# Reading a recurrent memory in products of 136 columns instead of a numerator and a denominator apart

## The chip, the cores and the metric

The kernel runs on one core of a Trainium2 chip. The metric is the device time of one execution in microseconds (us), as the median of several runs. A core has five engines that run their own instruction streams and wait for each other through semaphores: TensorE (PE in the profile, with its weight loads as PEld), VectorE (DVE), ScalarE (ACT), GpSimd (POOL) and SyncE (SP), which here only starts DMA transfers. TensorE writes its products into PSUM; VectorE and ScalarE read them from there.

## The reference

Two blocks read the same input `x` (2048 tokens of 512 numbers, bf16), and a gate per token mixes their outputs. Block A is attention with a memory: the tokens are cut into four segments of 512, there are 32 heads of 16 numbers, and each segment attends to itself causally and also reads a matrix `M` and a vector `z` that the earlier segments left.

```
for s in range(4):
    qs, ks, vs = q[:, :, s], k[:, :, s], v[:, :, s]
    p = softmax(qs @ ks^T * scale + mask)
    a_dot = p @ vs
    pq = phi(qs)
    num = einsum('bhld,bhde->bhle', pq, M)
    den = einsum('bhld,bhd->bhl', pq, z)[..., None] + 1e-06
    o = g * (num / den) + (1 - g) * a_dot
    pk = phi(ks)
    M = M + einsum('bhld,bhle->bhde', pk, vs)
    z = z + einsum('bhld->bhd', pk)
a = concat(o) @ wo                      # g = sigmoid(beta), phi(t) = t + 1 or exp(t)
b = (gelu(x @ w_gate) * (x @ w_up)) @ w_down
out = gx * a + (1 - gx) * b             # gx = sigmoid((x * gate_w).sum())
```

The memory of segment 0 is zero, so only segments 1 to 3 read it.

## The kernel before

Features lie on the partitions. The 32 heads are four groups `c` of eight heads, which fill the 128 partitions. For a segment, `QT`, `ktb` and `pq` hold the transposed queries, keys and phi of the queries, 512 tokens along the free side.

The attention of a group (a "lump") goes over 8 blocks of 64 keys. The work is cut into 72 visits, which the text calls periods 1 to 72: each computes the logits `lg` of one or two blocks (L653, four PSUM banks, one tile), takes their exponential on ScalarE (L658, `pT`), and clears what lies above the diagonal on GpSimd (L662). Two periods after its last block, the group's product with V goes into two PSUM tiles `od` (L678). VectorE turns them into `oq` (L684), a period or two later `norm` divides them by the sums of values (L689, L690, L692), `back` turns them to `oT` (L697), and `add_mem` adds what was read from the memory (L700).

All other products are units that fill the rest of TensorE's time in each period: `kT`, `qT`, `vT`, `zT` (projections), `gT` and `uT` (gate and up), `dT` (down, 14 products of 512 columns into one tile), `aT` (the output). Each writes one PSUM tile of one bank through `gen`, and VectorE or ScalarE then copies it out. The pool behind `gen` has four banks. A tile takes over the bank of an earlier one, and its first product waits until that one's readers are done. `od` takes two banks.

The order of the instructions is fixed when the program is built. A planner keeps an estimate of TensorE's and ScalarE's time (`t_pe`, `t_act`) and of VectorE's backlog (`passed(pe, dve)`), and starts units from the streams until the period's goal is reached (`fill_to`); `later(n, f)` puts a step n periods on; `room_for_bank` counts the banks taken while a unit is open, and finishes the unit after the third. A changed cost or a changed count of tiles therefore moves units everywhere. After period 72 the planner runs a stretch of fill, then the last lump (`od`, norm, back, add), then all that is left.

The memory: `memory(s)` adds a segment's sums to `Macc` (L566). `u_mask` spreads `Macc` into block-diagonal bf16 tiles, `Mz` for z (L582) and `Mn` for M (L574, four VectorE instructions a segment in two halves, two and eight periods later). `u_den` makes the denominators of two groups in one bank: eight products of 8 columns (L603, tile `zd`), then on VectorE the sum with 1e-6 (L610), a reciprocal (L613) and a product with the gate (L614), kept in `rdm`. `mem_num` makes a group's numerators: four products of 128 columns, one for each 128 tokens (L632, tile `mn`), one VectorE product with `rdm` (L636, `tm`), and a DMA transpose to `mT` (L644) on SP's queue, which also carries the output and the transposes of `pk`. `mem_num` of a group is asked for in the period before the group's last block, and issued in the middle of the next.

At the end, the four output units of segment 3 need all four groups in `oT`. Their first product that reads group 3 waits for the last L700.

Of the kernel before, what the change touches and what calls it, by code (L numbers as in the profile page):

```python
# [13 lines left out]
P = 128  # L14
# [39 lines left out]
def kernel(  # L54
# [44 lines left out]
    gh = const([P, H], F32, "gh")  # L99
# [114 lines left out]
    def setup_beta():  # L214
        eb = wk2.tile([P, H], F32, name="eb", tag="eb")
# [355 lines left out]
    def u_mask(s):  # L571
        def half(h0):
            for c in (h0, h0 + 1):
                nc.vector.tensor_tensor(  # L574
                    out=Mn[s % 2][:, c, :].rearrange("q (j p d) -> q j p d", j=4, p=2),
                    in0=Macc[:, c, None, :, 0:16].to_broadcast((P, 4, 2, DH)),
                    in1=bm[:, :, 0:16].rearrange("q (j p) d -> q j p d", j=4), op=ALU.mult)
            passed(0.0, 0.6)
            done["Mn", s] = count(("Mn", s)) + 1

        def f():
            nc.vector.tensor_tensor(  # L582
                out=Mz[s % 2][:, :, :].rearrange("q c (j p) -> q c j p", j=4),
                in0=Macc[:, :, None, :, 16].to_broadcast((P, NC8, 4, 2)),
                in1=bm[:, None, :, 16].to_broadcast((P, NC8, 8))
                .rearrange("q c (j p) -> q c j p", j=4), op=ALU.mult)
# [8 lines left out]
    def u_den(s, pair):  # L595
        def f():
            assert general_now[0] or ("q", s, 2 * pair) in ready
            T = gen("zd")
            Tv = T[:, 0:KT * 16].rearrange("p (q h) -> p q h", q=KT)
            for cc in range(2):  # L600
                c = 2 * pair + cc
                for qq in range(KT):
                    nc.tensor.matmul(Tv[:, qq, 8 * cc:8 * cc + 8],  # L603
                                     lhsT=pq[:, c, qq * P:(qq + 1) * P],
                                     rhs=Mz[s % 2][:, c, :], start=True, stop=True)
                if cc == 0:
                    yield 0.12
            h0 = 16 * pair
            r = rdm[s % 2][:, :, h0:h0 + 16]
            nc.vector.tensor_scalar_add(r, Tv, 1e-6)  # L610

            def f_inv():
                nc.vector.reciprocal(r, r)  # L613
                nc.vector.tensor_tensor(out=r, in0=r,  # L614
                                        in1=gh[:, None, h0:h0 + 16].to_broadcast((P, KT, 16)),
                                        op=ALU.mult)
                passed(0.0, 0.8)
                done["inv", s] = count(("inv", s)) + 1
            if general_now[0]:
                f_inv()  # L620
            else:
                later(1, f_inv)
            return 0.12
        return 0.24, 0.22, f

    tms = {}

    def mem_num(s, c):
        assert general_now[0] or (count(("Mn", s)) > c // 2 and count(("inv", s)) > c // 2)
        T = gen("mn")  # L630
        for qq in range(KT):
            nc.tensor.matmul(T[:, qq * P:(qq + 1) * P],  # L632
                             lhsT=pq[:, c, qq * P:(qq + 1) * P], rhs=Mn[s % 2][:, c, :],
                             start=True, stop=True)
        tm = wk2.tile([P, KT, 8, DH], BF, name="tm", tag="tm")
        nc.vector.tensor_tensor(  # L636
            out=tm[:, :, :, :], in0=T[:, :].rearrange("p (q h d) -> p q h d", q=KT, h=8),
            in1=rdm[s % 2][:, :, 8 * c:8 * c + 8, None].to_broadcast((P, KT, 8, DH)), op=ALU.mult)
        mT = wk2.tile([P, L], BF, name="mT", tag="mT")
        mTv = mT[:, :].rearrange("p (q t) -> p q t", q=KT)  # L640
        if general_now[0]:
            turn(mTv, tm[:, :, :, :].rearrange("p q h d -> p q (h d)"))
        else:
            nc.sync.dma_start_transpose(mTv, tm[:, :, :, :].rearrange("p q h d -> p (q h d)"))  # L644
        tms[(s, c)] = mT
# [21 lines left out]
    def pv(s, c, blocks):  # L667
# [14 lines left out]
        oq = wk2.tile([P, 2, 16, 32], F32, name="oq", tag="oq", bufs=1)  # L682
        for p in range(2):
            nc.vector.transpose(oq[:, p, :, :].rearrange("p b r -> p (b r)"), od[p][:, :])  # L684
        return oq

    def norm(c, oq, o2):
        rden = wk2.tile([P, 2, 16], F32, name="rden", tag="rden")
        nc.vector.reciprocal(rden[:, :, :], oq[:, :, :, 16])  # L689
        nc.vector.tensor_tensor(out=rden[:, :, :], in0=rden[:, :, :],  # L690
                                in1=ogs[:, c, :, None].to_broadcast((P, 2, 16)), op=ALU.mult)
        nc.vector.tensor_tensor(  # L692
            out=o2[:, :, :, :].rearrange("q b p d -> q p b d"), in0=oq[:, :, :, 0:16],
            in1=rden[:, :, :, None].to_broadcast((P, 2, 16, DH)), op=ALU.mult)
# [279 lines left out]
    def can_num(s, c):  # L974
        if count(("den", s)) <= c // 2 and ("q", s, c - c % 2) in ready:
            need(("den", s), c // 2 + 1)
        return count(("Mn", s)) > c // 2 and count(("inv", s)) > c // 2

    asked = []
# [12 lines left out]
    for pieces in visits:  # L992
# [51 lines left out]
    assert not asked  # L1044
# [59 lines left out]
    def general():  # L1104
# [4 lines left out]
        for s in range(NSEG):  # L1109
# [16 lines left out]
            if s > 0:  # L1126
# [3 lines left out]
                run(u_den(s, 0))  # L1130
                run(u_den(s, 1))
# [4 lines left out]
            for c in range(NC8):  # L1136
                o2 = wk2.tile([P, 16, 2, DH], BF, name="o2", tag="o2")
                if s > 0:
                    mem_num(s, c)
# [66 lines left out]
```

## Time and profile before

| | |
|---|---|
| median of 3 runs | 267.97 us (267.69 to 268.17) |
| the profiled execution | 267.87 us, of which 266.1 us from the first to the last instruction (the span) |
| VectorE busy | 202.2 us, 380 instructions |
| ScalarE busy | 208.8 us |
| GpSimd busy | 156.7 us |
| granted clock of TensorE | 0.998 |

In the rows of the groups, a line reads: line of the kernel, engine, operation, output<-input, sizes, count, then busy time in us and mean duration of one in ns, then idle time before it with what ended it. In rows in order of time: start and duration in us, engine, line, operation, count. Where a row has a count over one, its duration runs from the first start to the last end. Ends of matmuls are modelled: a product of 512 columns shows 0.38 us, but the next one starts 0.216 us after it.

### The profile page before, as it was taken

The numbers are of one execution on the slowest core, as the hardware profiler recorded it, in microseconds if no ns is written. First come the engines' busy times: TensorE is split into PE (matmuls) and PEld (weight loads), VectorE is DVE, ScalarE is ACT, GpSimd is POOL, SyncE is SP. The second block draws the span as 40 slices with busy tenths as digits, with TensorE's granted clock in tenths as the row PEclk, the third lists the DMA queues.
The fourth block names the chain that finished last, engine by engine and source line by source line (L and its number), as shares of the span: only waits on it lengthen the run. The fifth ranks groups of instructions, "written<-read, shape, count | busy, mean of one in ns | idle before, by whom it ended". The sixth has DMA issues, their size and how long they took to land.

```text
span 266.1 us, 6868 instructions
## 1 busy us (share of the span) xinstructions
PE 261.3 (98%) x2865; PEld 117.3 (44%) x2865; DVE 202.2 (76%) x380; ACT 208.8 (78%) x162; POOL 156.7 (59%) x298
## 2 busy tenths in 40 slices
PE   7999999999999999999999999999999999999994
PEld 4454434344443444443445444444444444444442
DVE  2999574978669887789786888786979647696565
ACT  4236889988998899979899998788999988757610
POOL 3000158896716979887941988874795099745500
PEclk9999999999999999999999999999999999999999
DMA  6999941200322001301132011201010210002102
GB/s 200 348 182 286 304 111 39 42 4 0 69 58 42 2 0 42 79 5 21 22 79 47 0 23 39 60 5 22 1 43 22 46 23 18 4 20 42 41 22 84
DMA packets 30410, 16.60 MB, mean 62 GB/s; under 512 B 20008, under 2 KB 29096, under 8 KB 30376
## 3 DMA queue, kind: packets, MB, share of 16 engines
q1 hardware_dynamic: 30232, 16.07, 23.8%
q8 instruction: 23, 0.38, 0.6%
q14 instruction: 11, 0.09, 0.1%
q10 hardware_dynamic: 144, 0.07, 0.1%
HBM read 8.14 MB, written 2.10 MB: 38 GB/s over the span
## 4 chain that ended last, share of the span: by engine, by line
PE 96%; DVE 2%; issue 1%; DVEq 0%
PE uT L493 19%; PE gT L472 19%; PE dT L509 17%; PE lg L653 9%; PE od L678 7%; PE kT L375 5%; PE qT L289 5%; PE aT L532 5%; PE vT L413 5%; PE mn L632 1%; PE warm L166 1%; PE zT L429 1%; PE MT L560 1%; DVE tB L538 1%; PE x0T L183 1%
## 5 line engine op out<-in xcount | busy, mean ns | idle before, releaser
L662 POOL TENSOR_SCALAR_AFFINE_SELECT pT<-pT 64x256 bf16<-64x256 bf16 x256 | 114.0, 445 | 92.8 <-ACT pT L658 80.2
L658 ACT ACTIVATE pT<-lg 128x2048 bf16<-128x2048 f32 x72 | 135.1, 1876 | 23.6 <-PE lg L653 22.1
L493 PE MATMUL uT<-x,wup 128*128 128x512 bf16 x224 | 59.6, 380 | 0.0
L472 PE MATMUL gT<-x,wga 128*128 128x512 bf16 x224 | 56.7, 380 | 0.0
L509 PE MATMUL dT<-wdn,G 128*128 128x512 bf16 x224 | 53.6, 380 | 0.0
L499 DVE TENSOR_TENSOR G<-uT,G 128x512 bf16<-128x512 f32 x56 | 37.8, 681 | 8.7 <-PE uT L493 8.4
L385 POOL TENSOR_SCALAR KTm<-ktb,eo 128x512 bf16<-128x512 bf16 x26 | 40.6, 1574 | 1.3
L684 DVE STREAM_TRANSPOSE oq<-od 128x512 f32<-128x512 f32 x32 | 21.0, 695 | 19.0 <-PE od L678 19.0
L509 PEld LDWEIGHTS <-G 128*128 128x128 bf16 x224 | 20.4, 98 | 24.3 <-issue 3.0
L472 PEld LDWEIGHTS <-wga 128*128 128x128 bf16 x224 | 20.5, 98 | 23.9 <-issue 2.4
L493 PEld LDWEIGHTS <-wup 128*128 128x128 bf16 x224 | 20.1, 98 | 24.4 <-issue 4.3
L653 PE MATMUL lg<-QT,KTm 32*128 32x192 bf16 (+7 forms) x512 | 28.6, 287 | 0.0
L312 DVE CAST G<-gT 128x512 bf16<-128x512 f32 x25 | 17.1, 684 | 5.5 <-PE gT L472 5.2
L653 PEld LDWEIGHTS <-KTm 32*128 32x128 bf16 x512 | 8.4, 92 | 29.2 <-issue 29.1
L487 ACT ACTIVATE G<-G 128x3584 bf16<-128x3584 bf16 x6 | 18.8, 3182 | 0.0
L678 PE MATMUL od<-pT,V 64*32 64x128 bf16 (+7 forms) x512 | 18.8, 284 | 0.0
L678 PE MATMUL od<-pT,Vs 64*32 64x128 bf16 (+7 forms) x512 | 18.7, 284 | 0.0
L375 PE MATMUL kT<-x,wk 128*128 128x512 bf16 x64 | 16.6, 379 | 0.4 <-DVE eo L204 0.4
L532 PE MATMUL aT<-wo,oT 128*128 128x512 bf16 (+1 forms) x72 | 16.8, 356 | 0.1
L289 PE MATMUL qT<-x,wq 128*128 128x512 bf16 x64 | 16.6, 379 | 0.0
L538 DVE SCALAR_TENSOR_TENSOR tB<-aT,gct,tB 128x512 bf16<-128x512 f32 (+1 forms) x18 | 11.9, 680 | 5.2 <-PE aT L532 2.7
L678 PEld LDWEIGHTS <-V 64*32 64x32 bf16 x512 | 12.8, 92 | 6.0 <-issue 2.8
(96 smaller groups left out, 273.4 us busy)
## 6 DMA issues: line engine op xcount, KB each, us to landing
wup<-in_B_w_up_dram SPq DMA_DIRECT2D x1, 1792.0 KB, 10.1
wdn<-in_B_w_down_dram SPq DMA_DIRECT2D x1, 1792.0 KB
out_dram<-tB SPq DMA_DIRECT2D x13, 128.0 KB, 1.7
wga<-in_B_w_gate_dram SPq DMA_DIRECT2D x1, 1280.0 KB, 10.3
Vs<-V SPq DMA_DIRECT2D x8, 144.0 KB, 2.9
G<-in_A_x_dram SPq DMA_DIRECT2D x2, 256.0 KB, 2.8
wk<-in_A_wk_dram SPq DMA_DIRECT2D x2, 256.0 KB, 4.3
wq<-in_A_wq_dram SPq DMA_DIRECT2D x1, 512.0 KB, 5.6
```

The costliest lines, as they stand in the source:

```text
L289: nc.tensor.matmul(T[:, :], lhsT=wq[:, fc, c * P:(c + 1) * P], rhs=xS[s % NX][:, fc, :], start=(fc == 0), stop=(fc == FC - 1))
L375: nc.tensor.matmul(T[:, :], lhsT=wk[:, fc, c * P:(c + 1) * P], rhs=xS[s % NX][:, fc, :], start=(fc == 0), stop=(fc == FC - 1))
L385: eng.tensor_scalar(out=KTm[:, (NC8 * s + c) % NK, :, p, :], in0=ktb[:, c, :].rearrange("q (b k) -> q b k", b=NB), scalar1=eo[:, p:p + 1], ...
L472: nc.tensor.matmul(T[:, :], lhsT=wga[:, fc, hs * P:(hs + 1) * P], rhs=xS[s % NX][:, fc, :], start=(fc == 0), stop=(fc == FC - 1))
L493: nc.tensor.matmul(T[:, :], lhsT=wup[:, fc, hs * P:(hs + 1) * P], rhs=xS[s % NX][:, fc, :], start=(fc == 0), stop=(fc == FC - 1))
L499: nc.vector.tensor_tensor(out=g, in0=T[:, :], in1=g, op=ALU.mult)
L509: nc.tensor.matmul(T[:, :], lhsT=G[s % NG][:, hs, qt * P:(qt + 1) * P], rhs=wdn[:, hs, :], start=(hs == 0), stop=(hs == HS - 1))
L532: nc.tensor.matmul(T[:, 0:w], lhsT=oT[:, fc, qt * P:(qt + 1) * P], rhs=wo[:, fc, d0:d0 + w], start=(fc == 0), stop=(fc == FC - 1))
L653: nc.tensor.matmul(lg[:, j, off:off + n], lhsT=KTm[rows, i % NK, b].rearrange("r p k -> r (p k)"), rhs=QT[rows, i % NC8, 64 * b:L], start= ...
L658: nc.scalar.activation(pT[:, :, :], lg[:, :, :], AF.Exp, scale=DH ** -0.5)
L662: nc.gpsimd.affine_select(out=v, in_=v, pattern=[[0, 4], [1, 64]], compare_op=ALU.is_ge, fill=0.0, base=0, channel_multiplier=-1)
L678: nc.tensor.matmul(od[p][32 * j:32 * j + 32, 64 * b:L], lhsT=w[:, 18 * h:18 * h + 32], rhs=t[rows, j, off:off + n], start=(b == 0), stop=( ...
```

## The change

- The denominators are no longer products of their own: `Mn` gets 136 columns, 128 of M and 8 of z, and one product makes both. Three products fill a bank (408 of 512 columns), so a segment's 16 products go into six tiles (`mem_read`, m = 0 to 5) instead of four `mn` and two `zd`. A tile of three may straddle two groups.
- VectorE now works on each tile as it comes: the sum with 1e-6 times `eb` (which is 1 + exp(-beta), the inverse of the gate) in one instruction, a reciprocal, and the product that writes `tm`. Where a tile straddles two groups, the first and the last come twice.
- The reads are asked for at other periods, and the planner books (0.18, 1.1) us for each.
- The four copies of `Macc` into `Mn` go from VectorE to GpSimd, without a cost in the planner; the eight columns of z stay on VectorE.
- `oq` is laid out as (block, parity, number) instead of (parity, block, number), so that `norm` reads and writes in one order.

```diff
-    Mn = [const([P, NC8, 128], BF, f"Mn{i}") for i in range(2)]
-    Mz = [const([P, NC8, 8], BF, f"Mz{i}") for i in range(2)]
-    rdm = [const([P, KT, H], F32, f"rdm{i}") for i in range(2)]
+    Mn = [const([P, NC8, 136], BF, f"Mn{i}") for i in range(2)]
...
-                nc.vector.tensor_tensor(
-                    out=Mn[s % 2][:, c, :].rearrange("q (j p d) -> q j p d", j=4, p=2),
+                nc.gpsimd.tensor_tensor(
+                    out=Mn[s % 2][:, c, 0:128].rearrange("q (j p d) -> q j p d", j=4, p=2),
...
-            passed(0.0, 0.6)
...
+    def mem_read(s, m):
+        T = gen("mn")
+        todo = [divmod(t, KT) for t in range(3 * m, min(3 * m + 3, NC8 * KT))]
+        rd = wk2.tile([P, 3, 8], F32, name="rd", tag="rd")
+        parts = []
+        for i, (c, qq) in enumerate(todo):
+            nc.tensor.matmul(T[:, 136 * i:136 * i + 136], lhsT=pq[:, c, qq * P:(qq + 1) * P],
+                             rhs=Mn[s % 2][:, c, :], start=True, stop=True)
...
+        for c, qq, i, n in parts:
+            nc.vector.scalar_tensor_tensor(
+                out=rd[:, i:i + n, :], in0=Tv[:, i:i + n, 128:136], scalar=1e-6,
+                in1=eb[:, None, 8 * c:8 * c + 8].to_broadcast((P, n, 8)),
+                op0=ALU.add, op1=ALU.mult)
+        nc.vector.reciprocal(rd[:, 0:len(todo), :], rd[:, 0:len(todo), :])
+        for c, qq, i, n in parts:
...
+            nc.vector.tensor_tensor(
+                out=tm[:, qq:qq + n, :, :],
+                in0=Tv[:, i:i + n, 0:128].rearrange("p q (h d) -> p q h d", h=8),
+                in1=rd[:, i:i + n, :, None].to_broadcast((P, n, 8, DH)), op=ALU.mult)
...
+                nc.sync.dma_start_transpose(mTv, tm[:, :, :, :].rearrange("p q h d -> p (q h d)"))
...
-        oq = wk2.tile([P, 2, 16, 32], F32, name="oq", tag="oq", bufs=1)
+        oq = wk2.tile([P, 16, 2, 32], F32, name="oq", tag="oq", bufs=1)
         for p in range(2):
-            nc.vector.transpose(oq[:, p, :, :].rearrange("p b r -> p (b r)"), od[p][:, :])
+            nc.vector.transpose(oq[:, :, p, :], od[p][:, :].rearrange("q (b r) -> q b r", b=16))
...
         nc.vector.tensor_tensor(
-            out=o2[:, :, :, :].rearrange("q b p d -> q p b d"), in0=oq[:, :, :, 0:16],
-            in1=rden[:, :, :, None].to_broadcast((P, 2, 16, DH)), op=ALU.mult)
+            out=o2[:, :, :, :], in0=oq[:, :, :, 0:16],
+            in1=rden[:, :, :, None].to_broadcast((P, 16, 2, DH)), op=ALU.mult)
...
-        us += [unit(u_den(s + 1, pair), NP * s + 16 + 9 * pair, ("den", s + 1),
-                    lambda s=s, pair=pair: ("q", s + 1, 2 * pair) in ready)
-               for pair in range(2)]
...
-    def numerator(s, c):
+    def read(s, m):
         room_for_bank()
-        mem_num(s, c)
-        done["num", s] = count(("num", s)) + 1
-        passed(0.3, EVAC)
+        mem_read(s, m)
+        passed(0.18, 1.1)
...
+    reads = [(last(NC8 * s + c) - back_, s, m) for s in range(1, NSEG)
+             for c, back_, m in ((0, 1, 0), (0, 0, 1), (1, 0, 2), (2, 0, 3), (3, 1, 4), (3, 0, 5))]
...
-        for i in range(NC8, NSEG * NC8):
-            if last(i) - 1 == clock[0]:
-                asked.append((i // NC8, i % NC8))
-        if asked and can_num(*asked[0]):
-            pending.append(lambda a=asked.pop(0): numerator(*a))
+        if reads and reads[0][0] <= clock[0] and can_read(*reads[0][1:]):
+            pending.append(lambda a=reads.pop(0)[1:]: read(*a))
```

More of the change, by code (lines that the diff above doesn't have):

```diff
@@ L582, in f @@
             nc.vector.tensor_tensor(
-                out=Mz[s % 2][:, :, :].rearrange("q c (j p) -> q c j p", j=4),
+                out=Mn[s % 2][:, :, 128:136].rearrange("q c (j p) -> q c j p", j=4),
                 in0=Macc[:, :, None, :, 16].to_broadcast((P, NC8, 4, 2)),
@@ L593, in u_mask @@
         return 0.0, 0.2, f
[L595 to L618, printed above, removed]
+    tms = {}
@@ L619, in f @@
             if general_now[0]:
-                f_inv()
+                turn(mTv, tm[:, :, :, :].rearrange("p q h d -> p q (h d)"))
             else:
[L622 to L645, printed above, removed]
@@ L647, in group_qk @@
+                nc.sync.dma_start_transpose(mTv, tm[:, :, :, :].rearrange("p q h d -> p (q h d)"))
+            tms[(s, c)] = mT
+            done["num", s] = count(("num", s)) + 1
     def group_qk(pieces):
@@ L966, in lump, with can_read @@
             later(4, f_add)
-    def numerator(s, c):
+    def read(s, m):
         room_for_bank()
-        mem_num(s, c)
-        done["num", s] = count(("num", s)) + 1
-        passed(0.3, EVAC)
[L974 to L979, printed above, removed]
+        mem_read(s, m)
+        passed(0.18, 1.1)
+    def can_read(s, m):
+        cs = {t // KT for t in range(3 * m, min(3 * m + 3, NC8 * KT))}
+        return all(count(("Mn", s)) > c // 2 and ("q", s, c - c % 2) in ready for c in cs)
+    reads = [(last(NC8 * s + c) - back_, s, m) for s in range(1, NSEG)
+             for c, back_, m in ((0, 1, 0), (0, 0, 1), (1, 0, 2), (2, 0, 3), (3, 1, 4), (3, 0, 5))]
     pending = []
@@ L1137, in general @@
                 o2 = wk2.tile([P, 16, 2, DH], BF, name="o2", tag="o2")
-                if s > 0:
-                    mem_num(s, c)
+                for m in ((0, 1), (2,), (3,), (4, 5))[c] if s > 0 else ():
+                    mem_read(s, m)
                 tiles = {}
```

26 lines of the change are left out of this document (19 added, 7 removed).

## The prediction

> **What bounds the kernel now.** I read the page's span and busy times first, then its chain, the stretches, the waits, and last the end in order of time.
>
> ```profile
> span 266.1 us, 6868 instructions
> PE 261.3 (98%) x2865; PEld 117.3 (44%) x2865; DVE 202.2 (76%) x380; ACT 208.8 (78%) x162; POOL 156.7 (59%) x298
> PE 96%; DVE 2%; issue 1%; DVEq 0%
> 160.00:230.00 70.00, 70.00 (x852) 31.27 (x836) 52.99 (x102) 60.97 (x45) 49.57 (x90) 1.00 0.12 27
> ```
>
> The last row is a stretch (length, then busy time of PE, PEld, DVE, ACT, POOL, with counts, granted clock). In the middle TensorE is busy 70.00 of 70.00 us at full clock, so each product removed from its stream is time saved, and each wait of its stream is time lost. The one wait of size is at the end:
>
> ```profile
> PEld L532 <- DVE oT L700: 0.6, 1, 0.6
> 254.82 4.28 PE L509 MATMUL dT<-wdn,G 128*128 128x512 bf16 x19
> 255.00 1.31 DVE L684 STREAM_TRANSPOSE oq<-od 128x512 f32<-128x512 f32 x2 [2.30 <-PE od L678]
> 256.24 0.67 DVE L697 STREAM_TRANSPOSE oT<-o 128x512 bf16<-128x512 bf16 x1
> 256.94 0.43 DVE L700 TENSOR_TENSOR oT<-oT,mT 128x512 bf16<-128x512 bf16 x1
> 257.89 0.69 DVE L692 TENSOR_TENSOR o<-oq,rden 128x512 bf16<-128x512 f32 x1
> 258.94 3.91 PE L532 MATMUL aT<-wo,oT 128*128 128x512 bf16 x24
> 259.36 0.42 DVE L700 TENSOR_TENSOR oT<-oT,mT 128x512 bf16<-128x512 bf16 x1
> ```
>
> The last lump's `od` ends at 254.82. VectorE then works without a gap until the last L700 ends at 259.78 (259.36 + 0.42), 4.96 us later. Meanwhile TensorE has 19 `dT` products (254.82 to 258.94, 0.217 each) and three of `aT` (0.65), 4.77 us. The fourth `aT` reads the last group, so TensorE stands still for some 0.25 us there. The end is set by where this `od` lies.
>
> **What is removed from TensorE.**
>
> ```profile
> 141.59 0.34 PE L603 MATMUL zd<-Mz,pq 128*128 128x8 bf16 x8
> 141.79 0.38 PE L289 MATMUL qT<-x,wq 128*128 128x512 bf16 x1
> 109.29 0.40 PE L653 MATMUL lg<-QT,KTm 32*128 32x512 bf16 x4
> 109.62 0.26 PE L603 MATMUL zd<-Mz,pq 128*128 128x8 bf16 x4
> 109.85 0.38 PE L493 MATMUL uT<-x,wup 128*128 128x512 bf16 x1
> L632 PE MATMUL mn<-Mn,pq 128*128 128x128 bf16 x48 | 4.6, 219 | 0.0
> ```
>
> Eight denominators take 0.20 us from start to the next unit's start (141.79 - 141.59), so the 48 take 6 x 0.20 = 1.2 us. The one unit that was cut by a logits group cost more: its last four took 0.23 instead of 0.10, so with its other half I count 0.2 extra. Removed: 1.4 us. Added: 48 products of 136 instead of 128 columns, at 0.216/512 per column 48 x 8 x 0.00042 = 0.16. Net -1.25. Their cost can't be much off; TensorE's row shows it whole.
>
> **What moves at the end.** In the order that the changed code builds, written as unit and count of products, period 72 and what follows it reads:
>
> ```
> before  dT7 mn4 dT7 aT4 dT9 od64 dT19 aT24
> after   aT2 dT5 mn3 dT9 aT4 dT7 mn1 dT7 od64 dT14 aT24
> ```
>
> The second read (`mn1`) takes a bank while a `dT` unit is open. With the two banks of `od` that is the third, so `room_for_bank` finishes the unit ahead of `od`: five products that lay behind `od` now lie before it. Behind it remain 14 x 0.217 + 0.65 = 3.69 us for VectorE's same 4.96 us; the wait grows from 0.25 to about 1.3. `od` ends 5 x 0.217 = 1.08 later, and the end with it: +1.08. The read itself is no part of this: its VectorE work (0.75, below) and L644 behind it on SP's queue end well before the add, since `mn1` lies 2.7 us of TensorE ahead of the end of `od` (dT7 1.5, `od` 1.2) and the add another 4.5.
>
> **What VectorE pays.** Removed: L574, L610, L613, L614, L636.
>
> ```profile
> L636 DVE TENSOR_TENSOR tm<-mn,rdm 128x512 bf16<-128x512 f32 x12 | 8.2, 680 | 0.6 <-PE mn L632 0.4
> L574 DVE TENSOR_TENSOR Mn<-Macc,bm 128x128 bf16<-128x128 f32 x12 | 3.9, 366 | 0.0
> L613 DVE RECIPROCAL rdm<-rdm 128x64 f32<-128x64 f32 x6 | 3.1, 523 | 0.0
> L614 DVE TENSOR_TENSOR rdm<-rdm,gh 128x64 f32<-128x64 f32 x6 | 1.5, 256 | 0.2
> L610 DVE TENSOR_SCALAR rdm<-zd 128x64 f32<-128x64 f32 x6 | 1.3, 209 | 0.0
> L538 DVE SCALAR_TENSOR_TENSOR tB<-aT,gct,tB 128x512 bf16<-128x512 f32 x14 | 10.3, 739 | 5.2 <-PE aT L532 2.7 <-ACT pT L658 2.2
> L437 DVE CAST V<-zT 128x128 bf16<-128x128 f32 x8 | 1.9, 280 | 0.0
> L689 DVE RECIPROCAL rden<-oq 128x32 f32<-128x32 f32 x16 | 5.4, 340 | 0.0
> L442 DVE COPY gct<-zT 128x4 f32<-128x4 f32 x4 | 0.6, 151 | 0.0
> ```
>
> That is 18.0 us of busy time. Added, with no row of their own: the sum on 24 numbers lies between a copy of 4 (151 ns) and the sum of 64 (209); I take 0.22. The reciprocal of 24 is below that of 32 (340) and above a third of L613's (0.17); I take 0.29. The product of 384 lies between 128 (280) and 512 (680), on the line between them 0.55, of 256 0.41. A read in one part (m 0, 3, 4) is then 0.22 + 0.29 + 0.55 and two hand-overs of 0.03 (256.24 + 0.67 to 256.94 above), 1.13 us; one in two parts (m 1, 2) has five instructions and takes 1.32, since neighbours that don't wait for each other overlap by 0.07 (255.00 + 1.31 to 256.24); m 5, 0.75. Bounds for one part are 0.9 and 1.3. Per segment 3 x 1.13 + 2 x 1.32 + 0.75 = 6.8, in all 20.4: VectorE gains no room, it does 2 us more.
>
> That by itself is hidden, since VectorE is idle 24% of the time. What isn't hidden is the **bank**: `mn` was free after one instruction of 0.68, and now is after the whole read. The rows of the one place of before where an `od` follows an `mn` into its bank:
>
> ```profile
> 214.83 0.39 PE L632 MATMUL mn<-Mn,pq 128*128 128x128 bf16 x4
> 215.05 0.38 PE L375 MATMUL kT<-x,wk 128*128 128x512 bf16 x1
> 215.25 0.69 DVE L636 TENSOR_TENSOR tm<-mn,rdm 128x512 bf16<-128x512 f32 x1
> 216.01 0.40 PE L653 MATMUL lg<-QT,KTm 32*128 32x448 bf16 x8
> 216.34 0.39 PE L678 MATMUL od<-pT,V 64*32 64x512 bf16 x1
> ```
>
> VectorE starts 0.20 after the last product ends (215.05), frees the bank at 215.94, and `od` starts at 216.34, 1.29 after the products: 0.40 to spare. In the changed order, three `od` stand as close behind an `mn` whose bank they take (units between `mn` and the logits group):
>
> ```
> period 24   aT4 gT1 mn3 gT3 uT1   then lg, od64     (m 1, two parts)
> period 33   vT4 uT1 mn3 uT3 gT1   then lg, od64     (m 3, one part)
> period 69   uT5 mn3 uT2 dT2       then lg, od64     (m 3, one part)
> ```
>
> ```profile
> L312 DVE CAST V<-vT 128x448 bf16<-128x448 f32 x9 | 5.5, 616 | 0.4
> 114.87 1.31 DVE L684 STREAM_TRANSPOSE oq<-od 128x512 f32<-128x512 f32 x2 [0.49 <-PE od L678]
> 125.07 0.75 DVE L538 SCALAR_TENSOR_TENSOR tB<-aT,gct,tB 128x512 bf16<-128x512 f32 x1 [0.28 <-PE aT L532]
> ```
>
> In each 0.86 us of products and the logits group lie between, as above, so 1.27 from `mn` to `od`. In period 24 VectorE has first to finish L538 of the `aT` that ended 0.40 before (0.20 + 0.75, in turn, so it begins the read 0.47 after `mn`): 0.47 + 1.32 + 0.08 to be seen - 1.27 = a wait of 0.60. In period 33 the copy of `vT` (0.62) stands ahead, and the read begins 0.34 after: 0.34 + 1.13 + 0.08 - 1.27 = 0.28. In period 69 it begins at 0.2: 0.14. Together 1.0, and with the bounds of a read 0.4 to 1.7. TensorE runs in order: behind the `od` stands everything else, the next logits group and so ScalarE's exponentials too. In period 46 (m 2) the sums of z and M stand between as well, 1.7 us: hidden by 0.1, and the first to bind if VectorE is later than I think.
>
> **GpSimd's copies.** No row shows one; by its rows for 512 numbers (1.57 us) and 136 with one input (0.38) a copy of 128 lies between 0.38 and 1.57, nearer the smaller by its size: 0.5, two at a time 1.0.
>
> ```profile
> L385 POOL TENSOR_SCALAR KTm<-ktb,eo 128x512 bf16<-128x512 bf16 x26 | 40.6, 1574 | 1.3
> L200 POOL TENSOR_SCALAR_AFFINE_SELECT bm<-bm 128x136 bf16<-128x136 bf16 x1 | 0.4, 382 | 0.1
> 123.52 2.01 POOL L662 TENSOR_SCALAR_AFFINE_SELECT pT<-pT 64x256 bf16<-64x256 bf16 x4 [0.71 <-ACT pT L658]
> 126.59 0.39 PE L678 MATMUL od<-pT,V 64*32 64x512 bf16 x1
> ```
>
> Behind them on POOL wait L662 and L385, and `od` waits for L662. The last row shows 0.71 us idle ahead of the masks, and they end at 125.53, 1.06 before the `od` at 126.59: 1.0 fits into the idle time and that distance. Nothing counted; if a copy took 1.57, three `od` (periods 16, 34, 52) would each wait 3.1 - 0.7 - 1.06 = 1.35. The Trainium skill (GPSIMD Engine Reference, Engine selection) says that GpSimd is about twice as slow as VectorE where an operation has two inputs; by it, from VectorE's quiet 0.28, a copy is an estimated 0.55 and the sum stays as it is.
>
> **The norm's order.** I count nothing, in either direction:
>
> ```profile
> L692 DVE TENSOR_TENSOR o<-oq,rden x16: 691/926/945, 50.9 to 257.9; 128x512 bf16<-128x512 f32 x16
> ```
>
> The same instruction takes 0.69 or 0.94; 0.69 is the pace of other products of 512. If the order were what costs the 0.25, up to 16 x 0.24 = 3.8 us of VectorE would go, and the three waits with it; at the end it is already 0.69, so the tail can't gain. The Trainium skill (GPSIMD Engine Reference, Key points) says that GpSimd shares its SBUF interfaces with VectorE, which suffers where it has two SBUF inputs; the norm has two, in either order. By that rule it stays at 0.94; the last one, with GpSimd done, is the quick one.
>
> **Sum**, against the profiled execution (267.87 us: span 266.1 and 1.8 around it; 0.10 below the median of the runs): 267.87 - 1.25 + 1.08 + 1.0 = 268.7, on the median's scale 268.8.
>
> **Rivals.**
> 1. *No bank wait*, because VectorE is ahead at the three places or the norm gives it 0.25 a lump: 267.87 - 1.25 + 1.08 = 267.7, on the median's scale 267.8, no change. For: before's closest case had 0.40 to spare. Against: 1.13 and 1.32 are longer than 0.69 by just this.
> 2. *The saving stays*: no waits, and the end hidden, as it would be if VectorE's last chain were 1.1 shorter: 267.97 - 1.25 = 266.7. Against: 4.96 us without a gap, with the norm at its quick pace already.
> 3. *VectorE falls behind* by 0.6 at each place, the 2 us more coming where it is busiest: the three waits grow to 2.8, period 46 waits 0.5: 268.8 + 2.3 = 271.1. It decides once the read begins 0.5 later than I have it. For: after a lump it can run without a gap for ten us (the rows at 114.87 and 125.07, the next that was idle before).
> 4. *GpSimd holds the masks up*, at 1.57 a copy: 268.8 + 3 x 1.35 = 272.8.
>
> **Numbers.** The forecast 0.47 (its own range, by the bounds of a read, 268.2 to 269.5), rival 1 0.22, rival 2 0.10, rival 3 0.16, rival 4 0.05. Range: 267.2 leaves out rival 2, 270.4 most of 3 and all of 4, together under 0.25 as rival 3 reaches down to 270. About 0.2% (0.54 us) can be told from no change. Faster: rival 2 and a little of rival 1, 0.14; the same: the rest of rival 1 and the forecast's low end, 0.25; slower: the rest, 0.61.
>
> **What would show it.** The L603 rows of `zd` gone and `mn` at some 0.06 a product; TensorE's waits naming `tm` or VectorE ahead of `od` in periods 25, 34 and 70; L532 waiting about 1.3 us for L700 at the end with 14 `dT` ahead; L692 still between 0.69 and 0.94; GpSimd's copies at 0.4 to 0.8. I am wrong if `od` starts without a wait in the middle, if a read is under 0.9 us, or if the last `aT` doesn't wait.

## The result, and the profile after

| | before | after |
|---|---|---|
| median, 4 runs each | 268.01 us (267.69 to 268.17) | 271.52 us (271.05 to 272.04) |
| the profiled execution | 267.87, span 266.1 | 272.04, span 270.2 |
| TensorE, first to last product's start | 261.60 | 265.71 |

After over before is 1.0131, with a 95% interval of 1.0109 to 1.0154: slower by 3.5 us. The forecast was 268.8, and 271.5 lies outside its range. The sign was right, the size was not. Some executions of several kernels are about 2 us longer than the rest of the same kernel (four each in runs 8, 11 and 13 below), without which, and without one of 1123.65 in run 8, the medians of these three would be 268.7, 268.1 and 268.2.

The page of the changed kernel: span, busy times, and the chain that ended last.

```profile
span 270.2 us, 6812 instructions
PE 262.5 (97%) x2817; PEld 116.7 (43%) x2817; DVE 202.7 (75%) x404; ACT 208.2 (77%) x162; POOL 161.2 (60%) x310
PE 88%; DVE 3%; POOL 3%; DMA 2%; issue 1%; ACT 1%; SPq 1%; DVEq 0%; POOLq 0%
```

TensorE's share of the chain fell from 96% to 88%. GpSimd, DMA and ScalarE are new in it, VectorE's share grew from 2% to 3%, and "issue", a wait for which the profile shows no releaser, is in it as before. The waits of TensorE, with total, count and longest, name the places:

```profile
PE aT L530 <- DVE oT L688: 1.2, 1, 1.2
PE gT L470 <- issue: 1.1, 1, 1.1
...
PE qT L287 <- DMA wq<-in_A_wq_dram: 0.2, 1, 0.2
PE od L666 <- POOL pT L650: 0.2, 1, 0.2
PE od L666 <- DVE tm L620: 0.2, 1, 0.2
```

This view shows too little. A product whose modelled span (0.38) reaches into the wait hides a part of it. The distances from each product's start to the next one's show it whole. Summed over the trace and split by place, they close the difference of 4.11 us:

| where | us |
|---|---|
| `zd` gone (-1.66, of which 0.30 returns: a product ahead of a logits group takes 0.10 longer, and three of those were `zd`) | -1.36 |
| `mn` with 136 columns (2.84 against 2.68) | +0.16 |
| second `od` tile of periods 25, 34, 70 | +0.56, +0.31, +0.43 |
| inside `od` of period 56, and of 61 | +0.92, +0.08 |
| inside a `gT` unit after `od` of period 47 | +1.29 |
| the last `aT` (1.35 against 0.27) | +1.08 |
| first `qT`, for the load of `wq` | +0.41 |
| a `uT` and the rest | +0.22 |

**Banks.** Period 24 and 25, rows of VectorE and of TensorE in order of time:

```profile
100.96 0.75 DVE L536 SCALAR_TENSOR_TENSOR tB<-aT,gct,tB 128x512 bf16<-128x512 f32 x1 [0.45 <-PE aT L530]
101.63 0.24 DVE L611 SCALAR_TENSOR_TENSOR rd<-mn,eb 128x8 f32<-128x8 f32 x2
101.90 0.30 DVE L615 RECIPROCAL rd<-rd 128x24 f32<-128x24 f32 x1
102.23 0.62 DVE L620 TENSOR_TENSOR tm<-mn,rd 128x128 bf16<-128x128 f32 x2
```

```profile
100.97 0.34 PE L603 MATMUL mn<-Mn,pq 128*128 128x136 bf16 x3
...
102.44 0.39 PE L666 MATMUL od<-pT,V 64*32 64x512 bf16 x1
103.00 0.37 PE L666 MATMUL od<-pT,Vs 64*32 64x512 bf16 x1 [0.18 <-DVE tm L620]
```

The products of `mn` end at 101.15, where the next unit starts. VectorE finishes L536 first, reads from 101.63 to 102.85, and only then is the bank free. The first `od` tile starts at 102.44, the second, which takes `mn`'s bank, 0.56 later.

**Masks.** GpSimd ahead of the `od` of period 56, which starts at 197.13:

```profile
191.67 2.15 POOL L650 TENSOR_SCALAR_AFFINE_SELECT pT<-pT 64x256 bf16<-64x256 bf16 x4 [0.49 <-ACT pT L646]
193.92 3.10 POOL L383 TENSOR_SCALAR KTm<-ktb,eo 128x512 bf16<-128x512 bf16 x2
196.98 2.79 POOL L650 TENSOR_SCALAR_AFFINE_SELECT pT<-pT 64x256 bf16<-64x256 bf16 x6
199.85 0.41 POOL L572 TENSOR_TENSOR Mn<-Macc,bm 128x128 bf16<-128x128 f32 x1
```

```profile
192.32 1.88 ACT L646 ACTIVATE pT<-lg 128x2048 bf16<-128x2048 f32 x1 [0.23 <-PE lg L641]
```

The exponential ends at 194.20, but its masks start at 196.98: a pair of `KTm` copies, 3.10 us, stands ahead of them. The copies of `Mn` come after, at 199.85, so they are not what is in the way.

**A wait without a releaser.** TensorE behind the `od` of period 47, and the DMA traffic of the stretch from 173.00 to 174.00 by queue (packets, MB, and the time of the packets as a share of 16 engines' time; packets that overlap can bring it over 100%):

```profile
173.68 0.61 PE L470 MATMUL gT<-x,wga 128*128 128x512 bf16 x2
175.41 0.59 PE L470 MATMUL gT<-x,wga 128*128 128x512 bf16 x2 [1.13 <-issue]
```

```profile
q1 hardware_dynamic: 499, 0.12, 152.3%
q8 instruction: 1, 0.02, 5.5%
```

The four products of one `gT` unit stand 1.5 us apart in their middle, with no data of their own to wait for. Just ahead, one 16 KB packet of instructions was fetched: it starts at 173.14 and takes 0.88 us.

A count places the stop. TensorE stops after its 1883rd product, which is after 3766 instructions, a weight load and a product each. The 21 other fetches of the trace, the last one left out, start between 24 instructions ahead of and 70 behind a count that lies a multiple of 256 from 3766; this one starts 188 behind. So the stop lies at the edge of a block of 256 instructions, and the edge before it lies two products into M's products.

**The end.**

```profile
258.93 3.19 PE L507 MATMUL dT<-wdn,G 128*128 128x512 bf16 x14
261.96 0.81 PE L530 MATMUL aT<-wo,oT 128*128 128x512 bf16 x3
263.95 3.00 PE L530 MATMUL aT<-wo,oT 128*128 128x512 bf16 x21 [1.18 <-DVE oT L688]
```

```profile
259.11 1.31 DVE L672 STREAM_TRANSPOSE oq<-od 128x512 f32<-128x512 f32 x2 [1.96 <-PE od L666]
...
263.47 0.42 DVE L688 TENSOR_TENSOR oT<-oT,mT 128x512 bf16<-128x512 bf16 x1
```

Fourteen `dT` and three `aT` lie behind `od`, VectorE needs the same 4.96 us as before (258.93 to 263.89), and the fourth `aT` waits: as forecast.

**What the new instructions take**, groups by form (busy, mean ns, idle before):

```profile
L620 DVE TENSOR_TENSOR tm<-mn,rd 128x384 bf16<-128x384 f32 x9 | 5.0, 557 | 0.3
L615 DVE RECIPROCAL rd<-rd 128x24 f32<-128x24 f32 x15 | 4.5, 303 | 0.5
L611 DVE SCALAR_TENSOR_TENSOR rd<-mn,eb 128x24 f32<-128x24 f32 x9 | 1.6, 173 | 0.9 <-PE mn L603 0.8
L572 POOL TENSOR_TENSOR Mn<-Macc,bm 128x128 bf16<-128x128 f32 x12 | 5.3, 459 | 0.5
L680 DVE TENSOR_TENSOR o<-oq,rden x16: 691/925/943, 51.3 to 262.0; 128x512 bf16<-128x512 f32 x16
```

### The profile page after: what moved, and what is told of

Same layout as the page of the kernel before. It is cut to its first block, busy times and chain, and to the rows that moved or that the text cites. A ratio compares the mean times of both kernels' runs of the same rounds, so it can differ in the third digit from the quotient of the medians.

```text
span 270.2 us, 6812 instructions
## 1 busy us (share of the span) xinstructions
PE 262.5 (97%) x2817; PEld 116.7 (43%) x2817; DVE 202.7 (75%) x404; ACT 208.2 (77%) x162; POOL 161.2 (60%) x310
## 4 chain that ended last, share of the span: by engine, by line
PE 88%; DVE 3%; POOL 3%; DMA 2%; issue 1%; ACT 1%; SPq 1%; DVEq 0%; POOLq 0%
PE uT L491 18%; PE gT L470 18%; PE dT L507 17%; PE lg L641 8%; PE od L666 6%; PE qT L287 5%; PE vT L411 5%; PE aT L530 4%; PE kT L373 4%; DMA wq<-in_A_wq_dram 2%; POOL pT L650 1%; POOL KTm L383 1%; PE mn L603 1%; DVE tB L536 1%; PE zT L427 1%
## 5 line engine op out<-in xcount | busy, mean ns | idle before, releaser
L491 PE MATMUL uT<-x,wup 128*128 128x512 bf16 x224 | 60.9, 380 | 0.0
L310 DVE CAST G<-gT 128x512 bf16<-128x512 f32 x28 | 19.1, 682 | 4.3 <-PE gT L470 3.9
L666 PE MATMUL od<-pT,V 64*32 64x128 bf16 (+7 forms) x512 | 20.3, 284 | 0.2 <-POOL pT L650 0.2
L666 PE MATMUL od<-pT,Vs 64*32 64x320 bf16 (+7 forms) x512 | 19.1, 284 | 0.3 <-DVE tm L620 0.2
L536 DVE SCALAR_TENSOR_TENSOR tB<-aT,gct,tB 128x512 bf16<-128x512 f32 (+1 forms) x18 | 11.9, 680 | 6.5 <-PE aT L530 6.3
L287 PE MATMUL qT<-x,wq 128*128 128x512 bf16 x64 | 16.0, 380 | 0.2 <-DMA wq<-in_A_wq_dram 0.2
L666 PEld LDWEIGHTS <-V 64*32 64x32 bf16 x512 | 13.5, 91 | 6.1 <-issue 2.9
```

What stands on the lines that cost most here:

```text
L287: nc.tensor.matmul(T[:, :], lhsT=wq[:, fc, c * P:(c + 1) * P], rhs=xS[s % NX][:, fc, :], start=(fc == 0), stop=(fc == FC - 1))
L491: nc.tensor.matmul(T[:, :], lhsT=wup[:, fc, hs * P:(hs + 1) * P], rhs=xS[s % NX][:, fc, :], start=(fc == 0), stop=(fc == FC - 1))
L666: nc.tensor.matmul(od[p][32 * j:32 * j + 32, 64 * b:L], lhsT=w[:, 18 * h:18 * h + 32], rhs=t[rows, j, off:off + n], start=(b == 0), stop=( ...
```

## The experiments

All start from the changed kernel unless said otherwise. The median of the kernel before, measured along with them, was 267.88 (runs 1 to 4), 268.05 (5 to 12), 267.81 (13, 14) and 267.98 (15, 16). Waits are distances between starts, less the product's own time.

### 1. Padding

```diff
+        for i in range(32):
+            nc.tensor.matmul(T[0:32, 0:8], lhsT=nc.const_aps.tensor(1.0, [64, 32], BF, 0), ...)
     transpose_x0()
+    pad()
```

> The changed kernel with 32 products of 8 columns (64 instructions) put into TensorE's stream after the turning of x, nothing else moved. In the profiled run of the changed kernel TensorE stood still for 1.13 us inside a gT unit at 175.4 with no releaser but 'issue'; the 16 KB block of instructions that it then needed had been fetched 2.2 us after the point at which its fetches normally come, because M's products and od (256 instructions in about 1.8 us) lie in one block. Theory A (the block's edge lies badly): the 64 instructions move the edge, the wait of 1.1 is gone, and the time is 271.5 - 1.1 + up to 0.4 for the products themselves (0.025 each, against 0.39 us idle there): 270.4 to 270.8. Theory B (a one-off of that execution): no such wait in this profile either, but the median of the timed runs stays at 271.5 to 271.9. Theory C (something the unit itself waits for): the wait stays at the same gT, 271.5 to 271.9.

Measured: 270.76, ratio 1.0127 (1.0086 to 1.0168). The `gT` unit behind that `od` has no gap:

```profile
171.55 0.67 PE L565 MATMUL MT<-V,pk 128*32 128x34 bf16 x64
173.25 1.04 PE L477 MATMUL gT<-x,wga 128*128 128x512 bf16 x4
```

In runs 2, 3, 4, 6, 7, whose instruction count is the same up to there, it stands at the same place with 0.86 to 1.31. So it is neither a one-off nor a wait of that unit for data: it hangs on how many instructions came before.

### 2. One KTm later

```diff
+            if clock[0] == 53:
+                later(3, mask_k)
+            else:
+                mask_k()
```

> The changed kernel with one pair of KTm copies (the kT unit of period 53) issued three periods later on GpSimd, nothing moved on TensorE. Theory A (the replanned kT put 3.1 us of KTm copies ahead of the masks that od of period 56 needs): the two waits inside that od (0.92 together) go, 271.5 - 0.9 = 270.6, and L650 no longer runs 6 in a row after L383 there. Theory B (GpSimd is held up by the change's copies of Mn or by VectorE): the od of period 56 still waits 0.5 us or more, 271.2 to 271.6.

Measured: 270.97, ratio 1.0110 (1.0090 to 1.0129). GpSimd at the same place:

```profile
191.38 2.16 POOL L656 TENSOR_SCALAR_AFFINE_SELECT pT<-pT 64x256 bf16<-64x256 bf16 x4 [0.48 <-ACT pT L652]
193.97 1.84 POOL L656 TENSOR_SCALAR_AFFINE_SELECT pT<-pT 64x256 bf16<-64x256 bf16 x4 [0.43 <-ACT pT L652]
```

The masks start with the exponential's end. The wait in period 56 falls from 0.92 to 0.21, that in 61 from 0.08 to none. Theory A, with 0.2 left over. The wait in period 70 came out at 0.64 here instead of 0.43, which takes a part of the gain.

### 3. A light read

```diff
-            nc.vector.scalar_tensor_tensor(out=rd[:, i:i + n, :], ..., op0=ALU.add, op1=ALU.mult)
-        nc.vector.reciprocal(rd[:, 0:len(todo), :], rd[:, 0:len(todo), :])
...
-                in1=rd[:, i:i + n, :, None].to_broadcast((P, n, 8, DH)), op=ALU.mult)
+                in1=eb[:, None, 8 * c:8 * c + 8, None].to_broadcast((P, n, 8, DH)), op=ALU.mult)
```

> The changed kernel without the sum and the reciprocal of a read (L611, L615): the product L620 takes eb in place of their result, so memory is not divided by its denominator. The read frees its bank after about 0.2 + 0.56 us instead of 1.1 to 1.3; TensorE's order is the same. Theory A (od waits for the bank of the read): the waits at the second od tile in periods 25, 34 and 70 (0.56, 0.31, 0.43) go, 271.5 - 1.3 = 270.2. Theory B (VectorE's work ahead of the read is what is late): at least half of the 1.3 stays, 270.8 or more.

Measured: 270.12, ratio 1.0076 (1.0052 to 1.0100). The kernel leaves out the division by the denominator. All three bank waits are zero, and the other waits stay (0.92 in period 56, 0.86 in `gT`, 1.35 at the end). Theory A.

### 4. The last lump's bank

```diff
-            while current and current[0][3][0] > 2:
+            while current and current[0][3][0] > most[0]:
...
+    most[0] = 3
     for _, i in lumps:
         lump(i)
```

> The changed kernel with the last lump allowed to take its bank while the open dT unit is unfinished: 7 dT products that lay ahead of the last od lie behind it, 21 instead of 14. Theory A (the end is set by where this od lies): the wait of the last aT for the add (1.3) goes whole, since 21 x 0.217 + 0.65 = 5.2 us now cover VectorE's 4.96: 271.5 - 1.3 = 270.2. Theory B (od then starts too early, and waits for masks, or the end moves by less): 270.8 to 271.5, with a wait at the od instead of at the aT.

Measured: 270.06, ratio 1.0084 (1.0062 to 1.0106).

```profile
256.81 4.71 PE L507 MATMUL dT<-wdn,G 128*128 128x512 bf16 x21
261.35 3.42 PE L530 MATMUL aT<-wo,oT 128*128 128x512 bf16 x22
```

21 `dT` behind `od`, and `aT` goes through without its wait. Theory A: this part of the forecast holds by intervention, not only by its row.

### 5. The same padding in the kernel before

> The kernel before with 28 products of 8 columns (56 instructions) put into TensorE's stream after the turning of x, nothing else moved. Counted in its order, the edge of a 256-instruction block then falls just ahead of M's products and the od of period 29, so that 282 instructions pass in an estimated 3.1 us there, as in the changed kernel at its 1.1 us wait (3.0 in its trace; the nearest of before has 5.6). Theory A (TensorE runs out of fetched instructions where the edge lies so): a wait of 0.7 to 1.3 us with the releaser 'issue' appears in the unit behind that od, at some 115 us, and the time is 267.9 + 1.0 = 268.6 to 269.2. Theory B (the wait has to do with something else that the change moved): no such wait, 267.9 to 268.2.

Measured: 268.23, ratio 0.9999 (0.9983 to 1.0016), and no wait: the expectation failed. The row of M's products and what follows it:

```profile
112.74 0.69 PE L567 MATMUL MT<-V,pk 128*32 128x34 bf16 x64
113.36 0.60 PE L500 MATMUL uT<-x,wup 128*128 128x512 bf16 x2
```

Two `uT` products stand between M's products and `od` here. In the kernel before something does in each of the two places (one `aT` in period 47); only in the new plan's period 47 do the two dense groups touch. The fetch starts 0.87 after M's products, where the changed kernel has 1.17, and ends at 114.53; TensorE goes from `dT` into the next logits group at 115.76, 1.23 later, without a wait. That the products in between make the room is argued, not shown: run 3's fetch starts only 0.38 after M's products, and TensorE waits 0.86 there.

### 6. The copies on VectorE

> The changed kernel with the 12 masked copies of memory on VectorE again, nothing moved on TensorE. Theory A (the copies on GpSimd cost the end nothing, as predicted): od of period 56 waits 0.9 as before and the time is 271.5, or up to 0.4 longer, where 0.37 us more a copy on VectorE lie ahead of a read. Theory B (the copies on GpSimd hold up the masks): the wait of period 56 and the one after it (0.92 and 0.08) shrink to under 0.3, 270.7 or less.

Measured: 272.09, ratio 1.0139 (1.0102 to 1.0175). Period 56 keeps its 0.94. Another `od`, at 89.1, now waits 0.26. The copies take less there,

```profile
L572 DVE TENSOR_TENSOR Mn<-Macc,bm 128x128 bf16<-128x128 f32 x12 | 3.5, 332 | 0.0
```

0.33 instead of 0.46, but on the engine that the banks wait for. Theory A by the wait of period 56: the move to GpSimd costs nothing there. The time lies 0.2 above what theory A allowed; that the move gains something is not shown, since the ratio can't be told from the changed kernel's 1.0131.

### 7. The norm's old order

> The changed kernel with the norm of before (sums of values as [2, 16, 32], the product's output turned instead), nothing moved on any engine. Theory A (the order costs nothing in either direction): the product keeps its 0.93 median and 0.69 at the end, the transposes their 0.70, and the time is 271.2 to 271.8. Theory B (the new order slows the transposes' output or speeds the product): one of the two changes by over 0.1 each, 1.6 us of VectorE or more, and the three bank waits with it, 0.3 or more on the time.

Measured: 271.56, ratio 1.0129 (1.0091 to 1.0166). The product has the same times (0.691, 0.926, 0.945 for least, median, most) as in the changed kernel (0.691, 0.925, 0.943), and the transposes have 0.696 in both. Theory A: the order does nothing in either direction.

### 8. Three repairs, planned anew

```diff
-        fill_to(t_pe[0] + 0.5 * (goal - t_pe[0]))
+        soon = bool(lumps) and lumps[0][0] == clock[0] + 1
+        fill_to(t_pe[0] + (0.0 if soon else 0.5) * (goal - t_pe[0]))
```

> The changed kernel with three repairs: the 32 padding products of the first run; the last lump's bank as in the fourth run; and, in a period ahead of a lump, the read issued at the period's start instead of halfway. Planned anew, the kT of period 53 also falls into period 54. If the four waits are what the change cost and are independent, 271.5 - 1.1 (fetch) - 1.3 (tail) - 1.3 (banks) - 0.9 (masks) = 266.9, faster than before by 1.0, which is what the removed products save. If the masks still wait behind the KTm copies: 267.8. If the repairs only move the waits: 268.5 or more.

Measured: 269.03, ratio 1.0050 (1.0025 to 1.0076): the repairs moved the waits. The planner put 28 `dT` straight behind the last `uT` of a segment, and `dT` now waits for the gated product behind a read:

```profile
139.15 0.29 DVE L627 TENSOR_TENSOR tm<-mn,rd 128x128 bf16<-128x128 f32 x1
139.35 0.68 DVE L504 TENSOR_TENSOR G<-uT,G 128x512 bf16<-128x512 f32 x1
```

1.0 us in two pieces. The `od` of period 70 still waits 0.50 with its read a period's half earlier: there VectorE has no gap for ten us, and the bank that is late is then that of a `uT`.

### 9 and 10. Repairs that leave the order alone

Run 9 has runs 1, 2 and 4, and issues the reads of periods 24 and 33 alone at their period's start. Run 10 also reads at 65 what was read at 69.

> The changed kernel with four repairs that leave the rest of TensorE's order as it is: the 32 padding products, KTm of period 53 three periods later, the last lump's bank as in the fourth run, and the reads of periods 24 and 33 at the period's start; the read of period 69 stays, since in the eighth run an od with its read moved ahead waited there all the same. If the waits are independent, TensorE's first product to last start comes to 265.7 - 1.3 - 0.8 - 1.35 - 0.9 = 261.4, against 261.6 of before, and the time to 267.5 to 268.2. If repairs open new waits, as in the eighth run: 268.6 or more.

> As the ninth run, and the third segment's read of period 69 issued in period 65, where VectorE has some two us idle ahead of it. Theory A (at period 70 the od waits because VectorE is behind by a whole read after ten us without a gap): the wait there (0.43 to 0.64) shrinks to under 0.15, and the time is 267.0 to 267.6, faster than before. Theory B (VectorE stays behind, since the read only joins the same gapless stretch earlier): the wait stays at 0.3 or more, 267.5 to 268.2.

Measured: 267.73, ratio 0.9996 (0.9982 to 1.0011), and 267.46, ratio 0.9992 (0.9967 to 1.0016). In both profiles a few matmul records are missing, and then a start lies 0.22 further off. With that taken off, the `od` of period 70 waits 0.63 (0.86 less 0.23) in the ninth and nothing in the tenth, for which theory A holds as far as this wait goes. Neither time can be told from that of the kernel before: both intervals hold 1.

### 11. More padding in the kernel before

> The kernel before with 110 products of 8 columns put in where the first run has 32; their own cost at the start is up to 110 x 0.025 - 0.4 = 2.4 us, read off the profile. By its order 282 instructions from the edge of a block then pass in 2.9 us at M's products and the od of period 47, less than the 3.35 at which the fifth run did not wait. Theory A (TensorE waits until about 1.25 us after the fetch's end, by all runs so far): a wait of 0.7 to 1.4 us named 'issue' in the unit behind that od, at some 171 us plus the cost at the start. Theory B (the fetch is not the cause): no wait there.

Measured: 268.34, ratio 1.0031 (1.0008 to 1.0054), no wait. The fetch starts 0.59 ahead of M's products, and the `aT` product stands between them and `od`. The expectation failed a second time.

### 12. The copies on GpSimd alone, in the kernel before

> The kernel before with its 12 masked copies of memory on GpSimd, nothing else: this part of the change alone. Theory A (hidden, as predicted): no wait of an od for masks over 0.1, 267.7 to 268.2. Theory B (they hold the masks up): an od of periods 16, 34 or 52 waits 0.3 or more, 268.4 or more.

Measured: 267.86, ratio 0.9993 (0.9983 to 1.0003). No `od` waits for masks:

```profile
L574 POOL TENSOR_TENSOR Mn<-Macc,bm 128x128 bf16<-128x128 f32 x12 | 4.9, 433 | 0.5
```

Theory A.

### 13. Six instructions less than in run 5

> The fifth run with 25 products of 8 columns instead of 28: 6 instructions fewer ahead of everything else. Its trace had the fetch start 0.3 us after the start of M's products of period 29, so the block's edge lay some 0.7 us, three products, ahead of them; now it falls on their start, and M's products and od, 256 instructions, pass in about 2.0 us instead of 2.98. Theory A (TensorE has the next block about 3.2 us after it enters one: 1.0 to the fetch's start, 0.95 of fetch, 1.25 until it goes on): a wait of 0.7 to 1.3 us after that od, at some 115 us, in a unit that had none, and 268.2 + 0.7 to 1.2 = 268.9 to 269.4. Theory B (something else of the changed kernel): no wait, 267.9 to 268.3 as in the fifth run.

Measured: 268.19, ratio 1.0029 (1.0004 to 1.0055), no wait in the profile. The fetch starts 0.31 after M's products, and not later, as the shift would have it. So the place of the edge alone doesn't tell when a fetch starts. (The expectation puts run 5's fetch 0.3 after M's products; in its trace it is 0.87.) The expectation failed a third time.

### 14. All repairs

As run 10, but the padding is in the warm-up and costs no columns:

```diff
-        for i in range(5):
-            nc.tensor.matmul(T[:, :], ..., rhs=nc.const_aps.tensor(1.0, [P, 512], BF), ...)
+        for i in range(25):
+            nc.tensor.matmul(T[:, 0:102], ..., rhs=nc.const_aps.tensor(1.0, [P, 102], BF), ...)
```

> The tenth run with the padding made in another way: the first warm-up as 25 products of 102 columns in place of 5 of 512, 40 instructions more at the same number of columns, so that no dense 256 instructions start nearer than 36 to an edge. Theory A (the four waits and the removed products are all there is): no wait over 0.3 on TensorE after the start, and 266.8 to 267.5, faster than before by 0.5 to 1.2. Theory B (what is left of the repairs is given back elsewhere): 267.6 to 268.2.

Measured: 267.32 (267.15 to 268.15) against 267.81, ratio 0.9986 (0.9977 to 0.9995): faster than the kernel before, by 0.5 us in the medians and by 0.1 to 0.6 us by the interval. So about half of the 1.2 us saved on products is kept at best; where the rest goes is shown only in part (0.21 in period 56, below).

```profile
span 265.6 us, 6849 instructions
PE 260.7 (98%) x2837; PEld 117.6 (44%) x2837; DVE 202.3 (76%) x404; ACT 207.9 (78%) x162; POOL 161.3 (61%) x310
...
PE 97%; DVE 1%; issue 0%; DVEq 0%
```

Period 56 keeps 0.21, the three bank waits are under 0.03, `gT` and the end have none. TensorE's first to last start is 261.11, against 261.60.

### 15 and 16. What the fetch hangs on

> The changed kernel without one transposing DMA of a read (mT of group 1 of the third segment, issued at 171.97 in the profiled run, 1.2 us before the late fetch starts); the add of that group takes group 0's mT instead, so memory's part of this group is left out. TensorE's instructions are the same. Theory A (the edge alone): the wait inside the gT unit behind od of period 47 stays, 0.8 to 1.3 us. Theory B (that DMA holds the fetch up): the fetch starts within 0.8 us of the edge, and the wait is under 0.5 us or gone.

> The changed kernel with 5 products of 8 columns (10 instructions) in the place of the first run's 32. The edge then lies 6 instructions, three products or 0.65 us, ahead of M's products, so that TensorE comes to the next edge in 2.6 us instead of 1.95. Theory A (a block is there about 3.2 us after the edge before it): the wait shrinks to 0.6 (0.4 to 0.8). Theory B (its length has nothing to do with the edge): 0.8 to 1.3 as in the other runs, or gone.

Measured: 271.42, ratio 1.0125 (1.0095 to 1.0154), and 270.56, ratio 1.0093 (1.0063 to 1.0122). Run 15's kernel leaves out memory's part of one group. Without that DMA the wait stays:

```profile
174.58 0.59 PE L470 MATMUL gT<-x,wga 128*128 128x512 bf16 x2 [0.81 <-issue]
```

One product of this unit has no record, ahead of the wait; with it the wait between starts is 0.77, just under the 0.8 of theory A and well over the 0.5 of theory B. So the DMA isn't what makes the wait. With 10 instructions more the wait is gone, not shortened to 0.6, though M's products and `od` still touch: the fetch starts 1.54 ahead of M's products, where the seven profiles with the wait have it 0.38 to 1.17 behind them. Theory A's rule for the length of the wait fails with that.

## Why the size was wrong, step by step

1. **What is removed.** Forecast -1.25 net, measured -1.36 + 0.16 = -1.20. Right.
2. **The end.** Forecast +1.08 with 14 `dT` behind `od`, measured +1.08 with 14. Right, and run 4 takes it away.
3. **The bank.** Forecast waits of 0.60, 0.28 and 0.14, together 1.0; measured 0.56, 0.31 and 0.43 (0.64 in some runs), 1.30. The mechanism and two of three sizes were right (run 3). The closeness of the first is in part luck: the read of period 24 takes 1.22 (101.63 to 102.85) and not 1.32, but `od` starts 0.15 after it and not 0.08. In period 69 I let VectorE begin the read 0.2 after the products; it begins 0.48 after them (243.43, where the next unit starts, to 243.91 in the trace), behind a gated product, and this makes the wait 0.43 instead of 0.14. Rival 3, VectorE behind by 0.6 everywhere, did not come, though its 271.1 lies nearest to the measured time: VectorE's busy time rose by 0.5, not by 2. The rows of the reads add up to 19.2, where the forecast's 20.4 held the hand-overs between instructions too, and a sum of 24 takes 0.17, not 0.22.
4. **GpSimd's copies: "Nothing counted".** Right for the copies: 0.46 each (forecast 0.5), and runs 6 and 12 show that they hold nothing up. Rival 4 asked the right question of the wrong instruction. The masks were late, in period 56, because the new plan put a `kT` unit into period 53, and its `KTm` copies of 3.1 us ahead of them (run 2).
5. **The norm's order.** Forecast nothing, measured nothing (run 7). That leaves open why the product takes 0.93 beside other work and 0.69 at the end, but neither kernel differs in it.
6. **The sum.** This is the step that failed. "267.87 - 1.25 + 1.08 + 1.0" adds what the reads and the last `od` do, and takes the rest of the new order for as good as the old. I had read the new order for one danger, an `od` close behind a read, and not for the two others: long copies that land ahead of masks on GpSimd (+1.0), and M's products and `od` side by side, 256 instructions that TensorE goes through faster than its next block comes (+1.29). Both stand in the order and could have been read from it. That the second costs something couldn't: no wait of this kind is in the trace of before.
7. What the median adds: 3.5 us. The terms found give -1.2 + 1.3 + 1.0 + 1.29 + 1.08 = 3.5. The 0.41 for the first `qT` belongs to the load of the one profiled execution; runs 1 and 2 show 0.16 and 0.13 there.

What stays open: what sets the start of an instruction fetch. Shown is that the wait follows the fetch (TensorE goes on 1.33 to 1.58 us after the fetch's end in all seven profiles with the wait), that it goes with 10 or 64 instructions more ahead of it, and that it stays without the transposing DMA beside it. Runs 5, 11 and 13 were to bring it into the kernel before, and none did; there one or two products stand between M's products and `od`, and whether that is why is not shown.

## What to carry to other kernels

Where TensorE has no idle time and a planner places the work, a removed product is worth its time only if the new order is read whole: for each engine that others wait for, look for the long instruction that moved ahead of a short one, and for each bank, who frees it last. Here a saving of 1.2 us was given back almost four times over by such places (1.3 + 1.0 + 1.29 + 1.08), and they were repaired one by one without replanning (run 14); the repair that let the planner run again moved them (run 8). Where many small instructions stand together, the count of instructions ahead of them is a cost of its own: test a pad before you explain a wait that names no releaser.

## What the runs showed of the hardware

- **Instruction fetch can stop TensorE.** TensorE's instructions come in packets of 16 KB (23 on queue q8 with 0.38 MB), one every 256 instructions or so, mostly 10 us apart. The 64 products of M and the 64 of `od`, each with its weight load, are 256 instructions in 1.71 us (171.97 to 173.68). With a fetch that started 0.38 to 1.17 after the first of them, TensorE stood still for 0.77 to 1.31. The Trainium skill (Runtime: NRT & Kernel Launch, Instruction fetch mechanics) says that the sequencer fetches blocks of 256 instructions itself, and that crossing a block's edge is mostly hidden. The size agrees with the packets; hidden it was not here.
- **GpSimd took less than twice VectorE's time in a small product of two inputs.** A copy of 128 with a mask takes 0.46 on GpSimd and 0.33 on VectorE (run 6), 1.4 to 1, and with the kernel before 0.43 (run 12) and 0.37, 1.2 to 1. The Trainium skill (GPSIMD Engine Reference, Engine selection) has about 2; the measurement decides.
- **TensorE can begin at half its pace.** The first twelve `kT` of run 12's profiled execution, and of the kernel before:

```profile
6.28 4.79 PE L375 MATMUL kT<-x,wk 128*128 128x512 bf16 x12 [0.39 <-DVE eo L204]
```

```profile
6.05 2.75 PE L375 MATMUL kT<-x,wk 128*128 128x512 bf16 x12 [0.39 <-DVE eo L204]
```

2.04 us more for the same products, start to start 0.43 instead of 0.216, while the granted clock's row says 1.00. That execution took 270.02 us where the median is 267.86, and run 13's profiled execution shows the same. What brings it about is not shown.
